# A kernel's prologue re-ordered: shorter TensorE filler, two x pieces summed together, the R4 sum moved ahead, transposes of group 1 moved ahead

## The chip, the core and the metric

The kernel runs on one core of a Trainium2 chip. The metric is the device time of one execution in microseconds (us). Five runs of the kernel before took 325.96, 326.41, 326.27, 325.49 and 325.08 us: median 325.96. One more execution was profiled; it took 325.05 us by the same clock. Below, TensorE is PE, VectorE is DVE, ScalarE is ACT, GpSimd is POOL, SyncE is SP. PEld is the loading of weights into TensorE, which the profile lists apart from the matmul.

## What is computed

Eight sequences (batches) of 4224 positions with 192 channels go through a causal convolution with softmax-normalised taps, then through a mixing block: a low-rank mix over the positions, and a two-layer network over the channels.

```python
w = softmax(weight, axis=-1)                       # 8 heads x 7 taps, 24 channels a head
y[b,s,h*24+g] = sum_k w[h,k] * x[b, s+k-6, h*24+g] # zero before the start
h = U^T y  (32 x 192), then  V^T h                 # rank 32 over the 4224 positions
u = y + V^T (U^T y)
out = u + relu(u @ w_ch1) @ w_ch2                  # 192 -> 768 -> 192
```

Inputs are float32; x, U, V and both channel weights are turned to bf16 by the transfers that load them, sums are held in float32, and the output is float32.

## The kernel before

A batch is 33 tiles of 128 positions, all eight batches 264 tiles, in 33 groups of 8 tiles. In steady work a group goes through three stages: `h_group` (V^T h from TensorE, added to y by DVE, giving u), a transpose of u, `w1` (36 matmuls of 512 columns, whose results pass through relu on ACT and DVE), and four calls of `w2` (24 narrower matmuls each pair of tiles, whose results DVE adds to u before SP stores them). The schedule is written out by hand: every engine runs its instructions in the order of the program, so what stands earlier in the text stands earlier in the queue. The list `SLOTS` orders everything after the prologue; the change does not touch it. It touches the prologue, which gets batch 0 from nothing to the first `w1`.

The names that matter there, with the lines of the kernel before:

- **x of batch 0** comes in four pieces (`KP`, L86, `x_piece`). A batch's x lies as two halves of 64 partitions, r = 0 (tiles 0 to 15) and r = 1 (tiles 16 to 32). Pieces 0 and 1 are the first ten tiles of each half, piece 2 the last 7 tiles of half 1, piece 3 the last 6 of half 0. POOL issues all loads (L79).
- **Filler**: `idle` (L153) multiplies a zeroed float32 tile `zz` (128x512, zeroed by DVE at L145) by its own first 128 columns. Each call appears as two passes in the trace. `idle(5)` stands first in TensorE's queue, `idle(1)` between the two band halves. Nothing reads the result.
- **The band matrices**: the convolution is a matmul with a banded weight matrix. DVE works from the taps to two products `pr` (L208), one for four heads each; `band_half` (L228) sums the 7 taps of one product on TensorE, and ACT (half 0) or DVE (half 1) copies the band out of PSUM in four pieces.
- **conv** (L351) computes the convolution for some heads and some tiles, and evicts the result to `y_sb`, an SBUF tile.
- **tt** is U^T y. `tt_mm` (L391) sums over tiles in four column strips of the array, four tiles at a time; the four partial sums are split into a bf16 head and rest (`tt_split`), and a matmul with `R4` adds the four and repeats the sum on all four strips. `tt_late` (L674) takes a tile by itself with the weights repeated four times over (`U4_sb`, made by POOL at L700), straight into the bank `ps0` where the final sum lies; it needs no R4. `tt_done` (L415) copies the sum to SBUF as `tt_sb`.
- **Groups 0 and 1** don't use the DMA transpose. `yT_part` (L498) transposes y of a piece of a group by matmuls with the identity; `hT_part` (L512) adds the transposed V^T h into the same PSUM bank, and evicts the sum to `uT`, the input of `w1`.

The order on TensorE before, after the first convolution: the U layout (L260), the first transposes of group 0, convolution of piece 2, `tt_mm` of the 20 tiles of pieces 0 and 1, convolution of piece 3, `tt_late` of the 7 tiles of piece 2, R4, `tt_late` of the 6 tiles of piece 3, the last transposes of group 0, `hT_part` of group 0, all transposes of group 1, `hT_part` of group 1, and then `w1` of group 0.

PSUM has 8 banks, handed out in turn by `bank()`.

Of the kernel before, what the change touches and what calls it, by code (L numbers as in the profile page):

```python
# [9 lines left out]
BF16 = mybir.dt.bfloat16  # L10
F32 = mybir.dt.float32
# [3 lines left out]
def kernel(  # L15
# [10 lines left out]
    nc = tc.nc  # L26
    P = nc.NUM_PARTITIONS
    B, S, D = x.shape
    H, KC = weight.shape
    GS = D // H  # L30
    R = moe_U.shape[1]
    M4 = moe_w_ch1.shape[1]
    NT = S // P
# [11 lines left out]
    cst = ctx.enter_context(tc.tile_pool(name="cst", bufs=1))  # L45
# [10 lines left out]
    def bank():  # L56
        return psp.tile([P, 512], F32, name="ps", tag="ps")
# [9 lines left out]
    NB0 = 32  # L67
    NB1 = S // HB - NB0
# [7 lines left out]
    def x_part(b, r, s0, s1):  # L76

        blk = NB0 * r + s0 - 1
        return nc.gpsimd.dma_start(  # L79
            out=xt[b][HB * r : HB * r + HB, s0:s1, :],  # L80
            in_=x[b, blk * HB : (blk + s1 - s0) * HB, :].rearrange("(j p) d -> p j d", p=HB),
        )

    XP = [(0, 1, 17), (0, 17, NB0 + 1), (1, 0, 18), (1, 18, NB1 + 1)]

    KP = [(0, 0, 10), (1, 0, 10), (1, 10, NB1 // 2), (0, 10, NB0 // 2)]  # L86

    def x_piece(k):
        r, k0, k1 = KP[k]
        x_part(0, r, (1 - r if k0 == 0 else 2 * k0 + 1), 2 * k1 + 1)  # L90

    def piece_tiles(k):
        r, k0, k1 = KP[k]
        return [NB0 // 2 * r + j for j in range(k0, k1)]

    x_tile(0)
    for k in range(2):
        x_piece(k)


    I32 = mybir.dt.int32
# [25 lines left out]
    )  # L127
    nlast = NT * 32 - nfull * P
    nc.gpsimd.dma_start(out=Ur[0:nlast, nfull, :], in_=U4[nfull * P :, :])
    for k in range(2, len(KP)):  # L130
        x_piece(k)


# [3 lines left out]
    for m0, m1 in ((0, 2 * P), (2 * P, M4)):  # L137
        for hf in range(2):
            nc.gpsimd.dma_start(
                out=W1_sb[HB * hf : HB * hf + HB, :, m0:m1],  # L140
                in_=moe_w_ch1[:, m0:m1].rearrange("(c k) m -> k c m", k=HB),
            )

    zz = cst.tile([P, 512], F32, name="zz")
    nc.vector.memzero(zz[:])  # L145

    rq = cst.tile([P, 2], F32, name="rq")
# [2 lines left out]
            nc.vector.memset(rq[QB * r : QB * r + QB, n : n + 1], v * r)  # L150
    wps = bank()

    def idle(n):  # L153
        for _ in range(n):
            nc.tensor.matmul(out=wps[:], lhsT=zz[:, 0:P], rhs=zz[:], start=True, stop=True)  # L155

    idle(5)

# [95 lines left out]
    def u_layout(up):  # L256
        nb = [nfull + (1 if 32 * jj < nlast else 0) for jj in range(4)]
        for a in range(4):
            for jj in range(4):
                nc.tensor.matmul(  # L260
                    out=up[jj][:, 0 : nb[jj] * R],
                    lhsT=Eq[32 * jj : 32 * jj + 32, a, :],
                    rhs=Ur[32 * jj : 32 * jj + 32, 0 : nb[jj], a * R : (a + 1) * R],
                    start=(a == 0),
                    stop=(a == 3),
                    tile_position=(32 * jj, 0),
                )
        for jj in range(4):
            evac(
                "AD"[jj % 2],  # L270
                U_sb[:, 0 : nb[jj], jj, :],
                up[jj][:, 0 : nb[jj] * R].rearrange("p (k r) -> p k r", r=R),
            )

    band_half(0)
    idle(1)
    band_half(1)


# [68 lines left out]
                    pp[part][:, 0 : nk[part] * GS].rearrange("p (k a) -> p k a", a=GS),  # L348
                )

    def conv(b, h0, nh, rs, engs, k0=0, k1=NT, pp=None):  # L351

        if yt[b] is None:
            yt[b] = ys.tile([P, NT, D], BF16, name="y_sb")
        nk = {r: min(k1, (NB0, NB1)[r] // 2) - k0 for r in rs}
        if pp is None:
            pp = {r: bank() for r in rs}
        w = nh * GS
        for hh in range(nh):
            h = h0 + hh  # L360
            for halo in range(2):
                for r in rs:
                    for c in range(2):
                        st = 1 - halo + c + 2 * k0
                        last = nc.tensor.matmul(  # L365
                            out=pp[r][HB * c : HB * c + HB, 0 : nk[r] * w].rearrange(
                                "p (k a) -> p k a", a=w
                            )[:, :, hh * GS : hh * GS + GS],
                            lhsT=bands[h // HQ][
                                HB * r : HB * r + HB, h % HQ, HB * halo : HB * halo + HB  # L370
                            ],
                            rhs=xt[b][
                                HB * r : HB * r + HB,
                                st : st + 2 * nk[r] - 1 : 2,
                                h * GS : h * GS + GS,
                            ],
                            start=(halo == 0),
                            stop=(halo == 1),
                            tile_position=(HB * r, HB * c),
                        )  # L380
        for n, r in enumerate(rs):
            j0 = NB0 // 2 * r + k0
            evac(
                engs[n % len(engs)],
                yt[b][:, j0 : j0 + nk[r], h0 * GS : h0 * GS + w],
                pp[r][:, 0 : nk[r] * w].rearrange("p (k a) -> p k a", a=w),
            )
        return last
# [3 lines left out]
    def tt_mm(b, js, p=None):  # L392

        if p is None:
            p = bank()
        for n, j in enumerate(js):
            c = n % 4
            nc.tensor.matmul(  # L398
                out=p[32 * c : 32 * c + 32, 0:D],
                lhsT=U_sb[:, j // 4, j % 4, :],  # L400
                rhs=yt[b][:, j, :],
                start=(n < 4),
                stop=(n + 4 >= len(js)),
                tile_position=(0, 32 * c),
            )
        return p

    def tt_split(b, p):

        hi = sml.tile([P, D], BF16, name="tt_hi")  # L410
        lo = sml.tile([P, D], BF16, name="tt_lo")
        nc.scalar.activation(out=hi[:], in_=p[:, 0:D], func=ACT.Copy)  # L412
        nc.vector.tensor_tensor(out=lo[:], in0=p[:, 0:D], in1=hi[:], op=ALU.subtract)
        ttb[b] += [hi, lo]
# [84 lines left out]
    def yT_part(g, parts):  # L499


        for c, i0, i1, p, _ in parts:
            for i in range(i0, i1):
                for hf in range(2):
                    nc.tensor.matmul(  # L505
                        out=p[HB * hf : HB * hf + HB, (i - i0) * P : (i - i0 + 1) * P],
                        lhsT=yt[0][:, GT * g + 4 * hf + i, HB * c : HB * c + HB],
                        rhs=ident[:],
                        start=(i == i0),
                        stop=False,  # L510
                        tile_position=(0, HB * hf),
                    )  # L512
# [156 lines left out]
        LOADS[b] = [(g, 0), (g, 3), (g + 1, 0), (g + 1, 3)]  # L669


    late = [piece_tiles(k) for k in (2, 3)]
    U4_sb = cst.tile([P, sum(len(js) for js in late), 4, R], BF16, name="U4_sb")

    def tt_late(p, js, o, first, last):

        for n, j in enumerate(js):
            nc.tensor.matmul(  # L678
                out=p[:, 0:D],
                lhsT=U4_sb[:, o + n, :, :].rearrange("p a r -> p (a r)"),  # L680
                rhs=yt[0][:, j, :],
                start=first and n == 0,
                stop=last and n + 1 == len(js),
            )

    def conv_piece(k, pps):
        r, k0, k1 = KP[k]
        for n, h in enumerate(range(0, H, 3)):
            conv(0, h, min(3, H - h), [r], "AD"[n % 2], k0, k1, {r: pps[n]})

    for h in range(0, H, 2):
        conv(0, h, 2, [0, 1], "AA" if h == 0 else "AD", *KP[0][1:])
    work = [bank() for _ in range(4)]
    u_layout(work)
    x_tile(1)
    x_zero(1, nc.gpsimd)
    x_part(1, *XP[0])
    o = 0
    for js in late:
        nc.gpsimd.tensor_copy(  # L700
            out=U4_sb[:, o : o + len(js), :, :],
            in_=U_sb[:]
            .rearrange("p k j r -> p (k j) r")[:, js[0] : js[-1] + 1, :]
            .unsqueeze(2)
            .to_broadcast([P, len(js), 4, R]),
        )
        o += len(js)

    NSL = (NT + 7) // 8 * 2
    V_sb = cst.tile([P, NSL, P], BF16, name="V_sb")  # L710
# [13 lines left out]
    W2_sb = cst.tile([P, MC, D], BF16, name="W2_sb")  # L724
    nc.gpsimd.dma_start(out=W2_sb[:], in_=moe_w_ch2[:].rearrange("(m p) d -> p m d", p=P))

    ps0 = bank()
    parts0 = [(0, 0, 2, bank(), "A"), (0, 2, 4, bank(), "D"), (1, 0, 4, bank(), "D")]
    yT_part(0, parts0)
    conv_piece(2, work[0:3])  # L730
    tt_mm(0, piece_tiles(0) + piece_tiles(1), work[3])
    tt_split(0, work[3])
    conv_piece(3, work[0:3])
    tt_late(ps0, late[0], 0, True, False)
    for part in ttb[0]:
        nc.tensor.matmul(out=ps0[:, 0:D], lhsT=R4[:], rhs=part[:], start=False, stop=False)
    tt_late(ps0, late[1], len(late[0]), False, True)
    more = [(2, 0, 2, bank(), "A"), (2, 2, 4, bank(), "A")]
    yT_part(0, more)
    tt_done(0, ps0)  # L740
    hT_part(0, parts0 + more)
    parts1 = [(c, 0, 4, bank(), "ADA"[c]) for c in range(3)]
    yT_part(1, parts1)
    hT_part(1, parts1)
    band2 = cst.tile([P, H, QB], BF16, name="band2")
    for xp in XP[1:]:
        x_part(1, *xp)
# [92 lines left out]
```

## Time and profile before

| | |
|---|---|
| median of 5 runs | 325.96 us (325.08 to 326.41) |
| the profiled execution | 325.05 us, of which the span from the first to the last recorded instruction is 323.3 us |
| outside the span | 1.75 us |
| DVE busy | 268.9 us (83%) |
| ACT busy | 170.4 us (53%) |
| POOL busy | 143.5 us (44%) |
| from 9.88 to 20.35 us (batch 0 up to the first `w1`) | PE 10.47 of 10.47 us busy, DVE 6.40, ACT 6.67, POOL 8.19; 194 GB/s moved |
| from 81 us on, each batch | about 28.1 us, PE busy throughout |

How to read it: a share of busy time is an average. The chain of waits says what set the end: it is followed back from the last instruction, step by step, to what released it. In the listings, a row gives the start in us from the span's beginning, the length in us, the engine, the line of the kernel, the operation, what it writes and reads, and how many; in brackets stands how long the engine sat idle ahead of it, and what ended that. A matmul's recorded length includes its way through the array, so rows overlap; the distance from start to start is what one costs in a stream.

### The profile page before, as it was taken

To read this page: it belongs to the slowest core of one execution; us is meant where nothing else is said; L and a number is where in the kernel's file an instruction comes from. 1 tells how busy PE (TensorE), PEld (TensorE's weight loads), DVE (VectorE), ACT (ScalarE), POOL (GpSimd) and SP (SyncE) were. 2 spreads that over 40 slices of the span, in tenths; PEclk is the share of its full clock that TensorE was granted. 3 is DMA by queue.
4 is the path that set the end of the run, shared out by engine and by line. 5 is a ranking of instruction groups with operands and counts; after the bars stand their busy time and mean duration, and the time that the engine had idled before them with its cause. 6 is when DMAs were issued, how large, how long until landed. Compare 5 with 4: busy or idle time off the path is not lost.

```text
span 323.3 us, 9590 instructions
## 1 busy us (share of the span) xinstructions
PE 318.1 (98%) x3998; PEld 224.0 (69%) x3998; DVE 268.9 (83%) x551; ACT 170.4 (53%) x344; POOL 143.5 (44%) x112
## 2 busy tenths in 40 slices
PE   8999999999999999999999999999999999999996
PEld 3757576478677647867864784587797497487495
DVE  7769989987977986998798699879888897896864
ACT  1766723860874397088339608824903902912920
POOL 8774179728957694785859497000000000000000
PEclk9999999999999999999999999999999999999999
DMA  9999993998998999699799957139269059048035
GB/s 104 193 192 183 207 212 101 190 194 257 211 134 202 226 175 172 168 153 199 171 235 150 223 150 196 37 111 242 58 170 270 3 149 269 25 121 271 2 120 175
DMA packets 122907, 53.52 MB, mean 166 GB/s; under 512 B 87760, under 2 KB 122832, under 8 KB 122864
## 3 DMA queue, kind: packets, MB, share of 16 engines
q1 hardware_dynamic: 84528, 38.08, 47.1%
q0 software_dynamic: 38192, 14.73, 40.1%
q8 instruction: 31, 0.51, 0.6%
q14 instruction: 12, 0.10, 0.1%
q10 hardware_dynamic: 144, 0.10, 0.1%
HBM read 29.49 MB, written 25.95 MB: 171 GB/s over the span
## 4 chain that ended last, share of the span: by engine, by line
PE 92%; ACT 3%; DMA 2%; DVE 1%; issue 0%; POOL 0%; POOLq 0%
PE ps L579 42%; PE ps L550 39%; PE ps L335 3%; PE ps L453 3%; DMA x_sb<-in_x_dram 2%; PE ps L398 2%; ACT rl_sb L564 2%; PE ps L365 1%; ACT y_sb L252 1%; PE ps L505 1%; DVE u_sb L475 1%; DVE rl_sb L566 1%; PE ps L520 0%; PE ps L678 0%; PE ps L424 0%
## 5 line engine op out<-in xcount | busy, mean ns | idle before, releaser
L564 ACT ACTIVATE rl_sb<-ps 128x512 bf16<-128x512 f32 x233 | 124.3, 604 | 108.0 <-PE ps L550 96.0
L579 PE MATMUL ps<-W_sb,rl_sb 128*128 128x192 bf16 x1584 | 141.9, 246 | 0.2
L579 PEld LDWEIGHTS <-rl_sb 128*128 128x128 bf16 x1584 | 128.1, 98 | 13.5 <-issue 13.1
L550 PE MATMUL ps<-uT,W_sb 64*128 64x512 bf16 x1188 | 131.7, 376 | 0.0
L566 DVE TENSOR_SCALAR rl_sb<-ps 128x512 bf16<-128x512 f32 x163 | 105.2, 686 | 15.7 <-PE ps L550 15.4
L550 PEld LDWEIGHTS <-W_sb 64*128 64x128 bf16 x1188 | 66.9, 94 | 60.5 <-issue 3.8
L588 DVE TENSOR_TENSOR out_sb<-ps,u_sb 128x384 f32<-128x384 f32 (+1 forms) x133 | 70.3, 548 | 25.9 <-PE ps L579 25.5
L301 POOL COPY xb_sb<-x_sb 32x3072 bf16<-32x3072 bf16 (+1 forms) x24 | 67.5, 2824 | 0.7
L475 DVE TENSOR_TENSOR u_sb<-y_sb,ps 128x192 bf16<-128x192 bf16 (+1 forms) x168 | 66.2, 459 | 0.0
L289 POOL COPY xb_sb<-x_sb 128x3072 bf16<-128x3072 bf16 x12 | 32.7, 2744 | 34.5 <-PE ps L335 24.8
L252 ACT ACTIVATE y_sb<-ps 128x384 bf16<-128x384 f32 (+4 forms) x90 | 38.2, 515 | 10.8 <-PE ps L335 7.8
L79 POOL DMA_DIRECT2D x_sb<-in_x_dram x32 | 27.0, 847 | 17.2 <-PE ps L550 10.4
L254 DVE CAST y_sb<-ps 128x408 bf16<-128x408 f32 (+4 forms) x36 | 19.1, 577 | 1.3 <-PE ps L365 1.1
L453 PE MATMUL ps<-tt_sb,V_sb 32*128 32x192 bf16 x264 | 12.4, 246 | 0.1
L335 PE MATMUL ps<-x_sb,band 64*32 64x384 bf16 x192 | 12.1, 333 | 0.0
L335 PE MATMUL ps<-xb_sb,band 64*32 64x384 bf16 x192 | 12.1, 332 | 0.0
L453 PEld LDWEIGHTS <-V_sb 32*128 32x128 bf16 x264 | 4.7, 92 | 7.3 <-issue 7.3
L155 PE MATMUL ps<-zz 128*128 128x512 f32 x12 | 7.2, 746 | 1.5 <-DVE zz L145 1.5
L365 PE MATMUL ps<-x_sb,band 64*64 64x240 bf16 (+3 forms) x192 | 8.0, 276 | 0.2 <-DMA x_sb<-in_x_dram 0.2
L412 ACT ACTIVATE tt_hi<-ps 128x192 bf16<-128x192 f32 x8 | 2.6, 330 | 10.6 <-PE ps L398 10.5
L335 PEld LDWEIGHTS <-band 64*32 64x32 bf16 x384 | 4.5, 89 | 4.1 <-issue 3.0
L365 PEld LDWEIGHTS <-band 64*64 64x64 bf16 x192 | 5.9, 106 | 2.2 <-issue 1.6
(65 smaller groups left out, 73.3 us busy)
## 6 DMA issues: line engine op xcount, KB each, us to landing
out_dram<-out_sb SPq DMA_DIRECT2D x131, 192.0 KB, 2.8
x_sb<-in_x_dram POOLq DMA_DIRECT2D x14, 384.0 KB, 7.6
x_sb<-in_x_dram POOLq DMA_DIRECT2D x7, 432.0 KB, 8.4
x_sb<-in_x_dram POOLq DMA_DIRECT2D x7, 408.0 KB, 7.6
x_sb<-in_x_dram POOLq DMA_DIRECT2D x1, 504.0 KB, 7.6
uT<-u_sb SPq DMA_TRANSPOSE x31, 4.0
x_sb<-in_x_dram POOLq DMA_DIRECT2D x1, 480.0 KB, 5.9
W_sb<-in_moe_w_ch_dram POOLq DMA_DIRECT2D x2, 192.0 KB, 7.5
```

Of the source, the lines that this page charges most:

```text
L79: return nc.gpsimd.dma_start(out=xt[b][HB * r : HB * r + HB, s0:s1, :], in_=x[b, blk * HB : (blk + s1 - s0) * HB, :].rearrange("(j p) d -> ...
L252: nc.scalar.activation(out=out, in_=in_, func=ACT.Copy)
L289: nc.gpsimd.tensor_copy(out=xbt[b][:, s0:s1, :], in_=xt[b][:, s0 + 1 : s1 + 1, :])
L301: nc.gpsimd.tensor_copy(out=xbt[b][q, s0:s1, :], in_=xt[b][q, s0:s1, :])
L335: nc.tensor.matmul(out=pp[r][QB * cg : QB * cg + QB, 0 : nk[r] * GS], lhsT=w[hr], rhs=t[hr, st : st + 2 * nk[r] - 1 : 2, hs], start=True, ...
L453: nc.tensor.matmul(out=banks[pr][:, a * D : (a + 1) * D], lhsT=V_sb[32 * q : 32 * q + 32, (j // 8) * 2 + j % 2, :], rhs=ttb[b][32 * q : 32 ...
L475: nc.vector.tensor_tensor(out=u_group(g)[:, i : i + n, :, hf, :], in0=yt[b][:, run[0] : run[0] + n, :].rearrange("p n (c k) -> p n c k", c=3),
L550: last = nc.tensor.matmul(out=pps[m][hf][:], lhsT=W1_sb[HB * hf : HB * hf + HB, c, m * P : (m + 1) * P], rhs=uTt[g][HB * hf : HB * hf + HB ...
L564: nc.scalar.activation(out=rl[:, m, hf, :], in_=pp[hf][:], func=ACT.Relu)
L566: nc.vector.tensor_scalar_max(out=rl[:, m, hf, :], in0=pp[hf][:], scalar1=0.0)
L579: last = nc.tensor.matmul(out=cps[:, a * D : (a + 1) * D], lhsT=rlt[g][:, m, hf, (i + a) * P : (i + a + 1) * P], rhs=W2_sb[:, m, :], start ...
L588: nc.vector.tensor_tensor(out=o[:, 0:n, :].rearrange("p n (c k) -> p n c k", c=3), in0=cps[:, 0 : n * D].rearrange("p (n c k) -> p n c k", ...
```

## The change

Five edits, all in the prologue.

1. The zero tile `zz` shrinks from 128x512 to 128x128, and the filler reads it four times over by a broadcast. `idle(5)` becomes `idle(4)`; the filler between the band halves is half as wide (256 columns).
2. Pieces 0 and 1 become one entry of `KP`; the four loads stay, in the same order.
3. `tt_mm` now takes 27 tiles: the 7 tiles of the third piece join the 20. `U4_sb` holds 6 tiles in place of 13, so one POOL copy goes (128x896; the one of 128x768 stays).
4. The R4 sum now opens the bank of the final sum, ahead of the late tiles; `tt_late` of 6 tiles follows. The final sum lies in `work[3]`, and `tt_mm` gets a bank `tp` of its own.
5. Of the last transposes of group 0, one half (4) goes between R4 and `tt_late`, the other stays behind it; 8 of the 24 transposes of group 1 move from behind `hT_part` of group 0 to in front of it.

On the engines other than TensorE, but for that one POOL copy, the order and number of the instructions stay as they were.

```diff
-    KP = [(0, 0, 10), (1, 0, 10), (1, 10, NB1 // 2), (0, 10, NB0 // 2)]
+    KP = [{0: (0, 10), 1: (0, 10)}, {1: (10, NB1 // 2)}, {0: (10, NB0 // 2)}]
...
-    zz = cst.tile([P, 512], F32, name="zz")
+    zz = cst.tile([P, P], F32, name="zz")
     nc.vector.memzero(zz[:])
...
-    def idle(n):
+    def idle(n, w=4):
         for _ in range(n):
-            nc.tensor.matmul(out=wps[:], lhsT=zz[:, 0:P], rhs=zz[:], start=True, stop=True)
-
-    idle(5)
+            nc.tensor.matmul(
+                out=wps[:, 0 : w * P].rearrange("p (n t) -> p n t", t=P),
+                lhsT=zz[:],
+                rhs=zz[:].unsqueeze(1).to_broadcast([P, w, P]),
+                start=True,
+                stop=True,
+            )
+
+    idle(4)
...
     band_half(0)
-    idle(1)
+    idle(1, 2)
     band_half(1)
...
-    late = [piece_tiles(k) for k in (2, 3)]
-    U4_sb = cst.tile([P, sum(len(js) for js in late), 4, R], BF16, name="U4_sb")
+    late = piece_tiles(2)
+    U4_sb = cst.tile([P, len(late), 4, R], BF16, name="U4_sb")
...
     work = [bank() for _ in range(4)]
+    tp = bank()
     u_layout(work)
...
-    ps0 = bank()
     parts0 = [(0, 0, 2, bank(), "A"), (0, 2, 4, bank(), "D"), (1, 0, 4, bank(), "D")]
     yT_part(0, parts0)
-    conv_piece(2, work[0:3])
-    tt_mm(0, piece_tiles(0) + piece_tiles(1), work[3])
-    tt_split(0, work[3])
-    conv_piece(3, work[0:3])
-    tt_late(ps0, late[0], 0, True, False)
-    for part in ttb[0]:
-        nc.tensor.matmul(out=ps0[:, 0:D], lhsT=R4[:], rhs=part[:], start=False, stop=False)
-    tt_late(ps0, late[1], len(late[0]), False, True)
+    conv_piece(1)
+    tt_mm(0, piece_tiles(0) + piece_tiles(1), tp)
+    tt_split(0, tp)
+    conv_piece(2)
+    ps0 = work[3]
+    for n, part in enumerate(ttb[0]):
+        nc.tensor.matmul(out=ps0[:, 0:D], lhsT=R4[:], rhs=part[:], start=(n == 0), stop=False)
     more = [(2, 0, 2, bank(), "A"), (2, 2, 4, bank(), "A")]
-    yT_part(0, more)
+    yT_part(0, more[0:1])
+    tt_late(ps0)
+    yT_part(0, more[1:])
+    parts1 = [(0, 0, 4, bank(), "A")]
+    yT_part(1, parts1)
     tt_done(0, ps0)
     hT_part(0, parts0 + more)
-    parts1 = [(c, 0, 4, bank(), "ADA"[c]) for c in range(3)]
-    yT_part(1, parts1)
-    hT_part(1, parts1)
+    rest = [(c, 0, 4, bank(), "ADA"[c]) for c in (1, 2)]
+    yT_part(1, rest)
+    hT_part(1, parts1 + rest)
```

More of the change, by code (lines that the diff above doesn't have):

```diff
@@ L84 @@
     XP = [(0, 1, 17), (0, 17, NB0 + 1), (1, 0, 18), (1, 18, NB1 + 1)]
-    KP = [(0, 0, 10), (1, 0, 10), (1, 10, NB1 // 2), (0, 10, NB0 // 2)]
+    KP = [{0: (0, 10), 1: (0, 10)}, {1: (10, NB1 // 2)}, {0: (10, NB0 // 2)}]
     def x_piece(k):
-        r, k0, k1 = KP[k]
-        x_part(0, r, (1 - r if k0 == 0 else 2 * k0 + 1), 2 * k1 + 1)
+        for r, (k0, k1) in KP[k].items():
+            x_part(0, r, (1 - r if k0 == 0 else 2 * k0 + 1), 2 * k1 + 1)
     def piece_tiles(k):
-        r, k0, k1 = KP[k]
-        return [NB0 // 2 * r + j for j in range(k0, k1)]
+        return [NB0 // 2 * r + j for r, ks in KP[k].items() for j in range(*ks)]
     x_tile(0)
-    for k in range(2):
-        x_piece(k)
+    x_piece(0)
     I32 = mybir.dt.int32
@@ L129 @@
     nc.gpsimd.dma_start(out=Ur[0:nlast, nfull, :], in_=U4[nfull * P :, :])
-    for k in range(2, len(KP)):
+    for k in range(1, len(KP)):
         x_piece(k)
@@ L349, in conv32, with conv @@
                 )
-    def conv(b, h0, nh, rs, engs, k0=0, k1=NT, pp=None):
+    def conv(b, h0, nh, rs, engs, ks=((0, NB0 // 2), (0, NB1 // 2)), pp=None):
         if yt[b] is None:
             yt[b] = ys.tile([P, NT, D], BF16, name="y_sb")
-        nk = {r: min(k1, (NB0, NB1)[r] // 2) - k0 for r in rs}
+        nk = {r: ks[r][1] - ks[r][0] for r in rs}
         if pp is None:
@@ L363, in conv @@
                     for c in range(2):
-                        st = 1 - halo + c + 2 * k0
+                        st = 1 - halo + c + 2 * ks[r][0]
                         last = nc.tensor.matmul(
@@ L381, in conv @@
         for n, r in enumerate(rs):
-            j0 = NB0 // 2 * r + k0
+            j0 = NB0 // 2 * r + ks[r][0]
             evac(
@@ L669, with tt_late @@
         LOADS[b] = [(g, 0), (g, 3), (g + 1, 0), (g + 1, 3)]
-    late = [piece_tiles(k) for k in (2, 3)]
-    U4_sb = cst.tile([P, sum(len(js) for js in late), 4, R], BF16, name="U4_sb")
-    def tt_late(p, js, o, first, last):
-        for n, j in enumerate(js):
+    late = piece_tiles(2)
+    U4_sb = cst.tile([P, len(late), 4, R], BF16, name="U4_sb")
+    def tt_late(p):
+        for n, j in enumerate(late):
             nc.tensor.matmul(
                 out=p[:, 0:D],
-                lhsT=U4_sb[:, o + n, :, :].rearrange("p a r -> p (a r)"),
+                lhsT=U4_sb[:, n, :, :].rearrange("p a r -> p (a r)"),
                 rhs=yt[0][:, j, :],
-                start=first and n == 0,
-                stop=last and n + 1 == len(js),
-            )
[L686 to L689, printed above, removed]
+                start=False,
+                stop=(n + 1 == len(late)),
+            )
     for h in range(0, H, 2):
-        conv(0, h, 2, [0, 1], "AA" if h == 0 else "AD", *KP[0][1:])
+        conv(0, h, 2, [0, 1], "AA" if h == 0 else "AD", KP[0])
     work = [bank() for _ in range(4)]
+    tp = bank()
     u_layout(work)
@@ L698 @@
     o = 0
-    for js in late:
+    for r, (k0, k1) in KP[2].items():
+        j = NB0 // 2 * r + k0
         nc.gpsimd.tensor_copy(
-            out=U4_sb[:, o : o + len(js), :, :],
+            out=U4_sb[:, o : o + k1 - k0, :, :],
             in_=U_sb[:]
-            .rearrange("p k j r -> p (k j) r")[:, js[0] : js[-1] + 1, :]
+            .rearrange("p k j r -> p (k j) r")[:, j : j + k1 - k0, :]
             .unsqueeze(2)
-            .to_broadcast([P, len(js), 4, R]),
+            .to_broadcast([P, k1 - k0, 4, R]),
         )
-        o += len(js)
+        o += k1 - k0
     NSL = (NT + 7) // 8 * 2
@@ L725, with conv_piece @@
     nc.gpsimd.dma_start(out=W2_sb[:], in_=moe_w_ch2[:].rearrange("(m p) d -> p m d", p=P))
-    ps0 = bank()
     parts0 = [(0, 0, 2, bank(), "A"), (0, 2, 4, bank(), "D"), (1, 0, 4, bank(), "D")]
     yT_part(0, parts0)
-    conv_piece(2, work[0:3])
-    tt_mm(0, piece_tiles(0) + piece_tiles(1), work[3])
-    tt_split(0, work[3])
-    conv_piece(3, work[0:3])
-    tt_late(ps0, late[0], 0, True, False)
-    for part in ttb[0]:
-        nc.tensor.matmul(out=ps0[:, 0:D], lhsT=R4[:], rhs=part[:], start=False, stop=False)
-    tt_late(ps0, late[1], len(late[0]), False, True)
-    more = [(2, 0, 2, bank(), "A"), (2, 2, 4, bank(), "A")]
-    yT_part(0, more)
+    def conv_piece(k):
+        for n, h in enumerate(range(0, H, 3)):
+            for r in KP[k]:
+                conv(0, h, min(3, H - h), [r], "AD"[n % 2], KP[k], {r: work[n]})
+    conv_piece(1)
[5 more added lines that the diff above has]
+        nc.tensor.matmul(out=ps0[:, 0:D], lhsT=R4[:], rhs=part[:], start=(n == 0), stop=False)
+    more = [(2, 0, 2, bank(), "A"), (2, 2, 4, bank(), "A")]
+    yT_part(0, more[0:1])
[3 more added lines that the diff above has]
+    yT_part(1, parts1)
     tt_done(0, ps0)
     hT_part(0, parts0 + more)
-    parts1 = [(c, 0, 4, bank(), "ADA"[c]) for c in range(3)]
-    yT_part(1, parts1)
-    hT_part(1, parts1)
+    rest = [(c, 0, 4, bank(), "ADA"[c]) for c in (1, 2)]
+    yT_part(1, rest)
+    hT_part(1, parts1 + rest)
     band2 = cst.tile([P, H, QB], BF16, name="band2")
```

## The prediction

> **What bounds the kernel now.** First the page's busy times and its chain of waits:
>
> ```profile
> PE 318.1 (98%) x3998; PEld 224.0 (69%) x3998; DVE 268.9 (83%) x551; ACT 170.4 (53%) x344; POOL 143.5 (44%) x112
> PE 92%; ACT 3%; DMA 2%; DVE 1%; issue 0%; POOL 0%; POOLq 0%
> ```
>
> TensorE's own work is 92% of the chain that sets the end. From 81 us on PE is busy throughout, so what the prologue saves on TensorE should arrive at the end, and what it saves elsewhere is worth nothing. So next the chain in order of time, for the first 45 us (start, length, what):
>
> ```profile
> 1.25 1.02 POOL x_sb L79
> 2.27 7.56 DMA x_sb<-in_x_dram
> ...
> 9.88 1.94 PE ps L365 x62
> 11.82 0.77 PE ps L260 x15
> 12.59 0.73 PE ps L505 x16
> 13.31 1.28 PE ps L365 x32
> 14.59 0.53 PE ps L398 x20
> 15.12 1.12 PE ps L365 x32
> 16.23 0.69 PE ps L678 x7
> 16.92 0.17 PE ps L736 x2
> 17.08 0.49 PE ps L678 x6
> 17.58 0.51 PE ps L505 x8
> 18.09 0.78 PE ps L520 x10
> 18.87 0.79 PE ps L505 x24
> 19.66 0.76 PE ps L520 x6
> 20.42 1.23 PE ps L550 x10
> ```
>
> The reader is to see two things. Up to 9.83 us the second x load holds the chain, not the band and not the filler; then TensorE runs without a gap to w1 at 20.42. Last, the filler's rows by tile (min/median/max ns) and the timeline around its end:
>
> ```profile
> L155 PEld LDWEIGHTS ps<-zz x12: 190/192/337, 1.5 to 7.9; 128*128 128x128 f32 x12
> L155 PE MATMUL ps<-zz x12: 592/592/1222, 1.5 to 8.4; 128*128 128x512 f32 x12
> 7.42 0.62 PE L232 MATMUL ps<-pr,ident 128*128 128x152 bf16 x7
> 8.79 0.62 PE L232 MATMUL ps<-pr,ident 128*128 128x152 bf16 x7
> ```
>
> **Filler and bands.** Ten filler passes run from 1.47 to 7.42. In the timeline they start at 2.48, 3.33, 4.19 (0.86 apart), then 4.85, 5.28, 5.71, 6.13 (0.43 apart): TensorE doubles its speed at about 4.65, since the weight loads halve as well (337 to 190 ns). The granted-clock column says 1.00 throughout and does not show this. The product for half 0 is there at about 7.3 (two products, 6.04 to 8.48, half each), so in this execution the filler delays half 0 by some 0.1. Half 1 starts at 8.79, its product ends at 8.48: 0.3 too late, of which DVE gives back little, being busy until 9.32 with other constants; its copies started at 9.45 and would start at 9.36. The second half of the first convolution waits for these copies (PEld idle 0.17 until the band), so it gains 0.09. But the third x piece was issued at 5.70 and landed 7.5 later, at 13.2, and its convolution began at 13.24: 0.00 to 0.09 is left. I take 0.04.
>
> **Other executions.** [...] The five runs reach from 325.08 to 326.41, median 325.96, and the profiled one, which switched early, took 325.05: 0.9 under the median. [...] With the change: clearing 128 columns in place of 512 takes about 0.17 in place of 0.485 (slope from the 256-column clears, 0.275 each), so passes start at 1.16; eight of them end at 6.4 if the speed doubles at 4.65, and at 8.1 at the latest (all slow). The half-width filler takes 0.43 at full speed. [...]
>
> [...]
>
> **27 tiles, R4 ahead.** Seven tiles in four strips cost 0.53/20 = 27 ns each, 0.19; as late tiles they cost 0.58 (16.17 to 16.75 in the timeline). They need the last eviction of their convolution piece, though (ACT, ends 15.09, against PE free at about 15.05): about 0.1 of wait. So the last convolution piece starts at 15.40 and ends at 16.52 in place of 16.23. R4 (0.17), then 4 transposes at 0.79/24 = 33 ns (0.13): 16.82. Now the 6 late tiles wait for the last eviction, which before started 0.05 behind the convolution and took 0.41: ready at 17.03, 0.2 of new wait on TensorE, with everything queued behind it. They end at 17.53 against 17.58. **Of the 0.39 saved on late tiles 0.05 is left**, because the eviction of the last piece is late next. The head/rest split on ACT and DVE moves 0.3 later and pushes the evictions behind it, which fit: DVE 15.84 to 16.2, then its copy 0.61, ready at 16.9.
>
> **Transposes of group 1.** Between the end of the late tiles and hT lies 0.51 (17.58 to 18.09), set by DVE's copy of the sum (0.36 and two hand-overs). Eight transposes of group 0 lay under it, 0.27. Now 12 do (4 and 8), 0.40: still covered, end at 17.93 against 18.04. Behind hT 16 remain in place of 24: **8 x 33 = 0.27 saved**. If that cover went, it would return as cost.
>
> **POOL and queues.** One copy goes: 896 of 1664 columns of 1.69 us, 0.91. The V loads behind it may issue that much sooner, at most; 4 x 64 KB is 1.35 us of traffic at 194 GB/s. That could push the last w_ch1 load, which landed at 11.78 + 7.2 = 19.0, to 19.5 at worst; w1 needs it after 21. The last V load waits for a w_ch1 load and stays at 17.74, landing at 23.4; h of group 2 would run at about 24.0 in place of 24.34. Covered, by 0.6. The x loads of batch 1 land at 31 and are used at 37.65. SP's order is unchanged. Each broadcast pass streams as many columns as before: nothing.
>
> **Sum** against the profiled execution: 0.04 + 0.05 + 0.27 = 0.36 (bounds 0.1, if the new waits double, and 0.6, if the evictions come as early as now); 325.05 - 0.36 = 324.7. From there I see no stage that takes it back: relu on ACT bounds 21.65 to 24.69, but starts when w1 starts. If the phase explains the runs, their median falls near the same value, plus 0.1 for late phases and landings: **324.8, 1.2 below 325.96**.
>
> **The cases.** A measurement of this kernel can tell about 0.3% (1.0 us) from no change.
>
> - *As forecast, 53%*: 324.8, own range 324.3 to 325.2.
> - *The phase doesn't matter, 27%*: spread has another source (transfer landings), only the sum counts: 325.96 - 0.36 = 325.6. For it: a single trace shows one switch; DMA engines are busy from 4 us on. Against: 0.9 between median and profiled run.
> - *The clock isn't open when the convolution starts, 12%*: one mechanism. [...]
> - *It doesn't do what it says, 8%*: the new waits on evictions take the whole 0.36 and the runs' spread stays: 326.0.
>
> A quarter of the first case and nearly all of the second and fourth lie within 0.3%. Faster by over 0.3% (below 324.98): three quarters of 53% and a little of the second, 0.44. Slower: 0.13. The rest, 0.43. The range leaves out the slow clock and the lower tail: 324.2 to 326.0.
>
> **What would show it.** In the trace after: filler starts at about 1.16 and TensorE has a gap ahead of the first band half; the second half begins near 8.5; the first convolution still begins when the x load lands; an idle of 0.1 ahead of the 21st tile of the 27 and 0.2 ahead of the late tiles, ended by ACT's eviction; w1 begins near 20.1. The five times should lie closer together than 1.3 us. Wrong if w1 begins no sooner, if band matmuls run at half pace, or if the times spread as before.

## The result and the profile after

The changed kernel takes 325.26 us (median of 28 runs, 325.02 to 327.12); the kernel before, run beside it, 325.42 us (47 runs, 324.80 to 327.99). Ratio 0.9995, 95% interval 0.9985 to 1.0006: no change that can be told. Under the median two things moved. The middle half of the runs drew together, from 325.05 to 326.08 before to 325.15 to 325.54 after; and the lowest time rose, from 324.80 to 325.02. One edit won, and another part of the change gave it back.

The profiled execution took 326.86 us, one of the slowest. The page's busy times and chain:

```profile
PE 318.1 (98%) x3996; PEld 221.7 (68%) x3996; DVE 268.5 (83%) x551; ACT 170.6 (52%) x344; POOL 142.8 (44%) x111
PE 87%; DMA 5%; DVE 3%; ACT 3%; issue 1%; POOL 0%; SPq 0%; DVEq 0%; POOLq 0%
```

PE is busy for the same time to 0.1 us. The chain's larger DMA share comes from one place far behind the change, seen in the chain in order of time:

```profile
71.57 0.04 SPq L600
...
71.70 7.75 DMA out_dram<-out_sb
```

That store took 7.75 us, against a median of 2.8, and DVE then waited for an output buffer. All other traces of this study have 304.70 to 304.74 us from the first matmul of w1 (in the timeline, where it starts 0.07 ahead of the chain's row) to the end of the time; this one has 306.13. So 1.4 us of it is this event, which no other trace repeats, and **for everything else the start of w1 tells the time**. The same view for the prologue:

```profile
2.28 7.60 DMA x_sb<-in_x_dram
9.88 0.04 issue
9.93 1.83 PE ps L369 x62
...
13.36 1.28 PE ps L369 x32
14.64 0.53 PE ps L402 x20
15.16 0.02 issue
15.18 0.34 PE ps L402 x7
15.53 1.12 PE ps L369 x32
16.65 0.27 PE ps L741 x2
16.92 0.23 PE ps L509 x4
17.15 0.04 issue
17.19 0.57 PE ps L682 x5
17.77 0.17 issue
17.93 0.24 PE ps L682
18.17 0.46 PE ps L509 x12
18.63 0.83 PE ps L524 x10
19.46 0.57 PE ps L509 x16
20.03 0.76 PE ps L524 x6
20.79 1.23 PE ps L554 x10
```

w1 starts at 20.79, not at 20.1, and later than the 20.42 of before. From the start of the third x piece's convolution, c3 for short (13.31 before, 13.36 here; ahead of it the landing of x sets the pace), it is 7.11 before and 7.43 now. The late tiles (L682) show why: five follow each other, then 0.17 of "issue", and only then the sixth, on whose sum DVE's copy and everything behind it wait. From start to start the fifth and sixth lie 0.41 apart; a late tile costs 0.08.

Two theories had to be tested. **C** (clock): the shorter filler makes the bands independent of the moment at which TensorE's speed doubles (4.64 in the trace of before, 4.07 in the changed kernel's). **F** (fetch): the gap is TensorE running out of instructions, at a fixed place of its stream. Rivals to F: **W**, a wait of the sixth tile for data; **S**, the loss lies only in the added switches of the array's tiling.

### The profile page after: what moved, and what is told of

Same layout as the page of the kernel before. It is cut to its first block, busy times and chain, and to the rows that moved or that the text cites. A ratio compares the mean times of both kernels' runs of the same rounds, so it can differ in the third digit from the quotient of the medians.

```text
span 325.0 us, 9584 instructions
## 1 busy us (share of the span) xinstructions
PE 318.1 (98%) x3996; PEld 221.7 (68%) x3996; DVE 268.5 (83%) x551; ACT 170.6 (52%) x344; POOL 142.8 (44%) x111
## 4 chain that ended last, share of the span: by engine, by line
PE 87%; DMA 5%; DVE 3%; ACT 3%; issue 1%; POOL 0%; SPq 0%; DVEq 0%; POOLq 0%
PE ps L583 39%; PE ps L554 38%; PE ps L339 3%; PE ps L457 3%; DMA out_dram<-out_sb 2%; DMA x_sb<-in_x_dram 2%; PE ps L402 2%; ACT rl_sb L568 2%; DVE u_sb L479 2%; PE ps L369 1%; ACT y_sb L256 1%; DVE out_sb L592 1%; DVE rl_sb L570 1%; PE ps L509 1%; PE ps L524 0%
## 5 line engine op out<-in xcount | busy, mean ns | idle before, releaser
L554 PEld LDWEIGHTS <-W_sb 64*128 64x128 bf16 x1188 | 65.0, 94 | 62.9 <-issue 4.5
L79 POOL DMA_DIRECT2D x_sb<-in_x_dram x32 | 27.1, 850 | 13.3 <-PE ps L554 6.6
L402 PE MATMUL ps<-y_sb,U_sb 128*32 128x192 bf16 x258 | 7.4, 247 | 0.0
```

Of the source, the lines that this page charges most:

```text
L79: return nc.gpsimd.dma_start(out=xt[b][HB * r : HB * r + HB, s0:s1, :], in_=x[b, blk * HB : (blk + s1 - s0) * HB, :].rearrange("(j p) d -> ...
L554: last = nc.tensor.matmul(out=pps[m][hf][:], lhsT=W1_sb[HB * hf : HB * hf + HB, c, m * P : (m + 1) * P], rhs=uTt[g][HB * hf : HB * hf + HB ...
```

## The experiments

The first four kernels were timed beside 51 runs of before (median 325.35 us), the last four beside 53 (325.51 us). "w1 behind c3" is the time in the trace from the first matmul of c3 to the first of w1; before 7.11.

| kernel | runs | lowest | median | middle half | ratio to before | w1 behind c3 |
|---|---|---|---|---|---|---|
| filler_only | 14 | 324.76 | 325.05 | 324.99 to 325.21 | 0.9994 (0.9982 to 1.0007) | 7.11 |
| order_only | 22 | 325.22 | 325.53 | 325.42 to 326.00 | 1.0014 (0.9999 to 1.0030) | 7.13 |
| halves_behind | 14 | 324.88 | 325.01 | 324.95 to 325.08 | 0.9992 (0.9977 to 1.0008) | 7.15 |
| pad16 | 14 | 324.86 | 325.65 | 325.06 to 325.79 | 1.0005 (0.9992 to 1.0018) | 7.10 |
| after_again | 13 | 325.06 | 325.19 | 325.13 to 325.33 | 0.9998 (0.9979 to 1.0017) | 7.39 |
| halves_pad8 | 14 | 324.98 | 325.47 | 325.13 to 325.66 | 0.9990 (0.9976 to 1.0005) | 7.25 |
| filler_c0 | 15 | 324.72 | 324.83 | 324.80 to 324.97 | 0.9981 (0.9972 to 0.9990) | 6.98 |
| no_filler | 20 | 325.25 | 326.12 | 325.64 to 326.56 | 1.0020 (1.0007 to 1.0033) | 7.11 |

Most intervals reach across 1, since the middle half of before is itself about 0.9 us wide; below, the traces carry the reading and the medians go beside them.

**filler_only**: before, with the first edit alone.

```diff
-    idle(5)
+    idle(4)
...
-    idle(1)
+    idle(1, 2)
```

> The kernel before with the first edit alone (smaller zero tile, 4 fillers in place of 5, a half-wide one between the band halves). Theory C (the filler holds the bands up in those executions where TensorE's speed doubles late): the first convolution starts when the x load lands in every execution, so the times lie within 0.8 us of each other and the median falls by about 0.5, to 324.9. Rival (the spread has another source, transfers): median and spread as before, 325.4 and 324.8 to 326.4. Theory F (TensorE's instruction stream runs dry at a fixed place, see the next run): four instructions fewer stand ahead, so the gap of 0.2 among the 8 transposes moves two transposes later, and w1 begins at 20.3 to 20.4.

As C has it: 13 of 14 times lie within 0.6 us (the other is 327.20), and the median is 325.05, less of a fall than the 324.9 expected. The floor hardly moves (324.76; before, timed beside it, 324.88), the upper half goes. The edit has three parts, a shorter clearing of `zz`, one filler less and a narrower one between the halves; no run takes them apart. As for F, the gap stands two transposes later, as expected, but is 0.05 long, and w1 began at 20.25.

**order_only**: the changed kernel with the old filler (the diff of filler_only turned round).

> The changed kernel with the filler of before (5 fillers, 512 columns, a full one between the halves): edits 2 to 5 alone. Theory F: the gap of 0.41 ahead of the sixth late tile comes from TensorE's instruction fetch and stands at a fixed count of instructions; four more stand ahead of it here, so it moves to the fourth late tile, and w1 begins at 20.7 to 20.8, as in the changed kernel. Rival W (the sixth late tile waits for an eviction or for its weights): the gap stays at the sixth. Theory C: the times spread over 1.3 us again, with a floor near 325.0 and a median near 325.8; without C the median is 325.2 to 325.4 with the narrow spread of the changed kernel.

Its trace happened to catch a late doubling. TensorE's timeline, then DVE's:

```profile
1.47 6.64 PE L153 MATMUL ps<-zz 128*128 128x512 f32 x10 [1.47 <-DVE zz L143]
7.94 0.62 PE L230 MATMUL ps<-pr,ident 128*128 128x152 bf16 x7
9.31 0.62 PE L230 MATMUL ps<-pr,ident 128*128 128x152 bf16 x7
...
11.33 1.01 PE L363 MATMUL ps<-x_sb,band 64*64 64x240 bf16 x30 [0.36 <-DVE band L252]
```

```profile
9.97 1.30 DVE L252 CAST band<-ps 32x152 bf16<-32x152 f32 x4 [0.64 <-PE ps L230]
```

The passes last 6.64 in place of 6.12, both band halves come 0.52 later than in the first trace (7.42 and 8.79), and now the convolution waits 0.36 for DVE's band, where it had been waiting for x. That is the loss which theory C supposes, seen, though in part made up again: of the 0.52, 0.18 is left at c3 (13.42 against 13.24 in the timeline). The median of 325.53, with a middle half 0.58 wide, lies between C's 325.8 and the 325.2 to 325.4 expected without C. That the longer times of before itself come from late doublings was not traced; it is inferred, since they go with the edit. Of F, the gap has moved to the fourth late tile as expected, but is 0.03 long, and w1 began at 20.62.

**halves_behind**: the changed kernel, transposes of group 0 back behind the late tiles.

```diff
-    yT_part(0, more[0:1])
     tt_late(ps0)
-    yT_part(0, more[1:])
+    yT_part(0, more)
```

> The changed kernel with the four transposes of group 0 that stood between R4 and the late tiles put back behind them. Theory S (a switch of the array's tiling between kinds of matmul costs 0.15 to 0.18 each, and the four transposes add two): R4 to late tile costs 0.08 again, and the late tiles are bound by ACT's last eviction. Theory F: the same number of instructions stands ahead of the gap, which now falls on the third transpose behind the late tiles and no longer on the sum; the copy of the sum starts at 17.65 in place of 18.21, w1 at 20.4 to 20.5 in place of 20.73, median about 325.0. Rival W: the gap stays with the sixth late tile, w1 at 20.7.

Here the speed doubled later still: the eight passes last 6.38, until 7.4, against 5.17 in the changed kernel's trace. With the new filler this costs nothing (TensorE's timeline):

```profile
1.07 6.38 PE L153 MATMUL ps<-zz 128*128 128x512 f32 x8 [1.07 <-DVE zz L143]
7.36 0.62 PE L236 MATMUL ps<-pr,ident 128*128 128x152 bf16 x7
...
8.54 0.62 PE L236 MATMUL ps<-pr,ident 128*128 128x152 bf16 x7
...
9.75 0.50 PE L369 MATMUL ps<-x_sb,band 64*64 64x240 bf16 x12 [0.37 <-DMA x_sb<-in_x_dram]
...
17.01 0.66 PE L682 MATMUL ps<-y_sb,U_sb 128*128 128x192 bf16 x6 [0.28 <-ACT y_sb L256]
```

Compare the second band half: 8.54 here and 9.31 in order_only. The last row shows the late tiles held by ACT's last eviction, as the prediction had it. No gap is left in this trace, and w1 comes 7.15 behind c3; the median is 325.01, 0.25 under the changed kernel's. Rival S finds no support: the first late tile starts 3.90 behind the first matmul of c3 here and in the changed kernel alike, so the two added switches delay nothing.

**pad16**: the changed kernel with four tiny float32 matmuls behind the first filler, 16 instructions in the stream.

```diff
     idle(4)
+    for _ in range(4):
+        nc.tensor.matmul(
+            out=wps[0:QB, 0:8], lhsT=zz[:, 0:QB], rhs=zz[:, 0:8], start=True, stop=True
+        )
```

> The changed kernel with four tiny float32 matmuls (sixteen instructions in the stream) added in the gap that TensorE has ahead of the bands, where they cost no time of their own. Theory F: the gap moves eight matmuls earlier, from the sixth late tile to the second or third of the four transposes behind R4, and is not shorter than before; w1 begins at 20.7 to 21.0. Rivals W and S: the place of the gap and w1 at 20.73 stay as they are. Median 325.2 to 325.5.

The gap left the sixth tile, against W; but none appeared at the new place, where F had expected one, and w1 came 7.10 behind c3, 0.3 sooner than in the changed kernel. The times fall in two clusters, 324.86 to 325.08 and 325.64 to 326.27 (and one of 327.33); the trace (325.06) is of the first, so what makes the second stays open.

**after_again**: the changed kernel, unchanged.

> The changed kernel once more, beside the next runs. Theory F (TensorE's instruction fetch is a race: it is asked for at a fixed place of the stream and lands about 2.4 us later, so the gap has the length by which TensorE comes too early): a gap of 0 to 0.4 ahead of the sixth late tile and nowhere else near, w1 begins 7.1 to 7.45 behind the convolution of the third x piece, median 325.25. If the gap in the first trace was a chance event: none here, 7.1, and the median above that of halves_behind needs another cause.

The chain in order of time has the gap at the same tile, and w1 7.39 behind c3:

```profile
17.12 0.57 PE ps L682 x5
17.69 0.12 issue
17.81 0.24 PE ps L682
```

**halves_pad8**: halves_behind with two of the tiny matmuls, 8 instructions, where TensorE waits for x.

```diff
     band_half(1)
+    for _ in range(2):
+        nc.tensor.matmul(
+            out=wps[0:QB, 0:8], lhsT=zz[:, 0:QB], rhs=zz[:, 0:8], start=True, stop=True
+        )
```

> halves_behind with two tiny float32 matmuls (eight instructions) between the second band half and the first convolution, where TensorE waits for x anyway. Theory F: the place at which the stream can run dry moves four matmuls earlier, from the fourth transpose behind the late tiles to the sixth late tile itself, so the sum is late again: median 325.2 to 325.3 against 325.01, with a gap of 0 to 0.4 ahead of the sixth late tile in the trace. Rival S (what halves_behind won came from the two switches of the array's tiling alone): the median stays at 325.0.

The gap is back on the sixth late tile, which starts 0.18 behind the fifth. In TensorE's timeline the six tiles last 0.75, against 0.66 in halves_behind:

```profile
16.89 0.75 PE L686 MATMUL ps<-y_sb,U_sb 128*128 128x192 bf16 x6 [0.28 <-ACT y_sb L256]
```

The median is 0.46 above that of halves_behind, more than F asked, but before, timed beside each, differs by 0.16, and the ratio to before shows no rise (0.9990 against 0.9992). This trace, at 324.98 us, is the quickest of its runs, so it does not show the rest; the padding itself may have a share in it.

All traces together: the start of the first 16 KB packet of the instruction queue (q8), the moment at which TensorE would have gone on at the place in question (the 446th of the instructions in the trace, weight loads and matmuls counted alike; a float32 matmul is two of each), the gap, and the time from the packet's start to TensorE's going on, in us.

```
kernel         packet   place reached   gap    packet to go-on
before          15.39   17.51           0.20   2.32
changed         15.50   17.60           0.33   2.43
after_again     15.35   17.53           0.29   2.46
order_only      15.08   17.57           0.03   2.52
filler_only     15.20   17.42           0.05   2.27
filler_c0       15.13   17.37           0.05   2.30
halves_pad8     15.10   17.30           0.10   2.30
halves_behind   15.38   17.68           none
pad16           14.35   16.79           none
no_filler       15.88   18.80           none
```

In seven traces, of six kernels, the gap stands at the 446th instruction, wherever that falls: on the second transpose before, on the sixth or fourth late tile, on the fourth transpose. It ends 2.3 to 2.5 us behind the packet's start; the three traces without a gap reach the place 2.30, 2.44 and 2.92 behind it. On the sum the gap costs its whole length: 0.33 and 0.29 in the two traces of the changed kernel put w1 at 7.43 and 7.39, where pad16, with the same order and no gap, has 7.10; 0.10 in halves_pad8 puts it at 7.25, where halves_behind has 7.15. The trace of before had it too, 0.20 long; there it fell on transposes under DVE's copy of the sum, and cost nothing (7.11, as in filler_only with 0.05). Theory F holds for the place; W falls. The page of the changed kernel has 31 packets of 0.51 MB together for q8, of kind "instruction", so 16 KB each, and 3996 matmuls and as many weight loads for TensorE, some 8000 instructions. That q8 serves TensorE is inferred from these counts, and that the packet is what TensorE waits for from the times; no run changed the packet itself. The moment of the packet's start is not at a fixed count: between 320 and 374 instructions had begun by then. And the size of the effect on the medians is shown less well than its place.

**filler_c0**: filler_only and, of the fifth edit, only the eight transposes of group 1 moved ahead of hT of group 0.

```diff
     yT_part(0, more)
+    parts1 = [(0, 0, 4, bank(), "A")]
+    yT_part(1, parts1)
     tt_done(0, ps0)
     hT_part(0, parts0 + more)
-    parts1 = [(c, 0, 4, bank(), "ADA"[c]) for c in range(3)]
-    yT_part(1, parts1)
-    hT_part(1, parts1)
+    rest = [(c, 0, 4, bank(), "ADA"[c]) for c in (1, 2)]
+    yT_part(1, rest)
+    hT_part(1, parts1 + rest)
```

> The kernel before with the first edit and of the fifth edit only the move of 8 transposes of group 1 to the front of hT of group 0; R4, the late tiles and the 20-tile sum as before. TensorE has 0.12 to spare there beside the switch; the eight add 0.21 to 0.25 in front and take 0.22 away behind. If the cover is as the trace of filler_only has it, w1 begins 0.1 sooner against the convolution of the third x piece (7.0 in place of 7.11), median 324.95. If the copy of the sum doesn't cover them: 7.1, 325.05.

w1 comes 6.98 behind c3, and the median of 324.83 beats both kernels: ratio to before 0.9981 (0.9972 to 0.9990), the filler's gain included, and 0.36 us under the changed kernel timed beside it (after_again). The chain in order of time:

```profile
16.87 0.49 PE ps L684 x6
17.36 0.62 PE ps L511 x16
17.98 0.77 PE ps L526 x10
18.75 0.57 PE ps L511 x16
19.32 0.76 PE ps L526 x6
20.08 1.23 PE ps L556 x10
```

Sixteen transposes stand under the copy of the sum for 0.62, where eight had 0.51; the sixteen behind cost 0.57 in place of 0.79. Net 0.11, a gap of 0.05 included: of all that was tried with the order, only this move gained. halves_behind differs from this kernel only by the 27-tile sum with R4 ahead (edits 2 to 4), and has 7.15: **the 27-tile sum with R4 ahead costs 0.17**.

**no_filler**: the changed kernel without any filler.

```diff
-    idle(4)
...
-    idle(1, 2)
```

> The changed kernel without any filler; nothing that the output needs is left out. Theory C: TensorE is still at half speed when the bands are made at 7.4 and when the convolution starts, until about 3 us to 6.5 us of work behind 7.4; w1 begins 1.5 to 3 us later, median 326.7 to 328.3. Rival (the filler is of no use, the halved speed belongs to the start of the program): w1 at 20.4 and a median near 325.2.

The median is 326.12, 0.9 above after_again. TensorE's timeline:

```profile
9.52 3.46 PE L367 MATMUL ps<-x_sb,band 64*64 64x240 bf16 x64
```

The first convolution takes 3.46 in place of about 1.9; from the U layout on the pace is normal. So the filler is of use, but the loss is below the expected 1.5 to 3: the slow stretch ended within this convolution (the trace's record of the granted clock begins at 12.72, 5.3 behind the first band matmul), and of the 1.2 by which it ends later than in the changed kernel, 0.4 is made up ahead of c3, which started at 14.1 in place of 13.3. Its w1 comes 7.11 behind c3 although the order is the changed kernel's: with 20 instructions fewer ahead, the 446th lies among the transposes behind the late tiles, and no gap shows.

## Why the prediction was right or wrong

The range held because it reached up to no change: 325.26 is 0.46 above the likeliest value, 324.8, and none of the four cases came out as written. The runs drew together, as in the first; new waits took the order's saving, as in the fourth. That the time fell inside is owed to the width of the range more than to the sum: by the prediction's own sign, "Wrong if w1 begins no sooner", the half on the order failed, since w1 began 0.37 later (20.79 against 20.42). Step by step:

- **Filler and bands, other executions: right in mechanism, too large.** The changed kernel's two traces have the doubling at 4.07 and 5.45, the nine traces with a filler between about 4.1 and 7.1, that is 3.0 to 6.0 behind the first pass. So the same kernel meets it at different moments; what sets them, no run shows. With the old filler a late one moves the bands (order_only, where the second half starts at 9.31 in place of 8.79), with the new one it doesn't (halves_behind; in every trace with the new filler the second half starts at 8.53 or 8.54). But the gain was read from the median of five runs, 325.96, against one trace at 325.05, 0.9 apart. With 47 runs the median of before is 325.42. The edit is worth about 0.3 in the median (before to filler_only, 325.35 to 325.05; order_only to the changed kernel, 325.53 to 325.26). The 0.1 that the sum adds for late phases, that is late doublings, and landings is shown by no run: with the new filler the second half starts at the same 8.53 or 8.54 however late the doubling.
- **27 tiles, R4 ahead: the step that failed.** The late tiles were to end 0.05 sooner than before. Where no gap disturbs them they end 0.22 later, counted from c3: 4.49 in halves_behind (17.67 less 13.18) and in pad16 (17.79 less 13.30), against 4.27 before (17.58 less 13.31). The largest part of this miss of 0.27 lies in "They end at 17.53", which allows the six tiles 0.50 from their start at 17.03. That is the chain's 0.49, which counts from the end of the matmul ahead; from the first one's start to the last one's end, the timeline of before has 0.66:

```profile
16.92 0.66 PE L678 MATMUL ps<-y_sb,U_sb 128*128 128x192 bf16 x6
```

Behind a wait no other matmul hides the first one's way through the array, and the six cost the full 0.66, as the row of halves_behind shows: 0.16 of the miss. Another 0.08 is the last piece's convolution, which starts 0.36 later (15.53 less 13.36, against 15.12 less 13.31) and not 0.28: the 21st tile starts 0.27 behind the 20th, where rows of four tiles lie 0.08 apart, so the wait there is 0.19 and not 0.1. The rest, about 0.03, is the hand-over from ACT.
- **The four transposes behind R4: mispriced, without effect.** "R4 (0.17), then 4 transposes (0.13)" took 0.50. Transposes were priced at the pace of a long run, 33 ns. But the array is tiled otherwise for the transposes (128*64 in the rows) than for R4 and the late tiles (128*128), and in these traces the first matmul of another tiling comes later: the trace before has 0.175 from the last late tile to the first transpose, where two late tiles lie 0.082 apart, and in the changed kernel the transposes start 0.176 behind R4. Yet this did not make the sum late. ACT's last copy of the convolution sets the late tiles, in the changed kernel (first row) as in halves_behind (second), where nothing stands between:

```profile
16.06 1.04 ACT L256 ACTIVATE y_sb<-ps 128x432 bf16<-128x432 f32 x2 [0.16 <-PE ps L369]
15.88 1.04 ACT L256 ACTIVATE y_sb<-ps 128x432 bf16<-128x432 f32 x2 [0.16 <-PE ps L369]
```

The copies end at 17.10 and 16.92, and the late tiles start 0.09 later in both, at 17.19 and 17.01.
- **A gap that no wait explains.** "They end at 17.53" failed by a further 0.29 to 0.33 in the changed kernel: the sixth late tile has no such row in the profile before, where the gap fell on covered work. The text called the queues harmless after looking at the transfers of data; the instruction queue q8 was left out.
- **Transposes of group 1: right, a little smaller.** Twelve lie under the copy for 0.46, and 16 behind cost 0.57 in place of 0.79: 0.22 against the stated 0.27.
- **Sum.** The order was to save 0.32 (0.05 and 0.27). It loses 0.22 ahead of the sum and wins 0.22 behind it, so it is worth about nothing where no gap falls on the sum (7.10 to 7.15 behind c3 against 7.11), and costs 0.28 to 0.32 where the whole gap does. With the 0.3 that the filler won, this leaves the median where it was. "No stage that takes it back" was right: w1's start carried to the end within 0.04 us in every trace but the one with the slow store.
- **The clock that isn't open**: did not come about in any trace with a filler. With the latest doubling, 7.1 in filler_c0, the eight passes last until 7.7, the bands follow without a gap, and the first convolution's 62 matmuls take 1.94, as before. Only no_filler has the convolution start at the slow pace, and it lost 0.9 in the median.

## What to carry to other kernels

When a change puts a group of short matmuls behind a wait, count it from its first start to its last end, as its row in the timeline has it, and not by its share of a chain in which rows overlap (here 0.66 against 0.49). Count a change of array tiling too (here 0.15 to 0.2 from start to start, against 0.03 to 0.08 within a kind), where no later wait covers it. Keep what the next stage waits for away from a place where the traces show such a gap (here the 446th instruction), or leave covered work there: 0.20 us of it cost nothing on transposes (before), while 0.29 and 0.33 us on the sum cost their whole length (the changed kernel's two traces). And take the size of a gain in spread from many runs: five had put the median 0.5 too high.

## What the runs showed of the hardware

- The instruction queue q8 moved 31 packets of 16 KB, in 0.6% of the time of the 16 DMA engines that also moved the data (9 tenths busy in the page's second and third slices, 8 to 24 us). In the seven traces with a gap TensorE would have gone on at the 446th instruction 2.1 to 2.5 us behind the start of the first packet, and did go on 2.3 to 2.5 us behind it, 0.03 to 0.33 us late. That the two race each other is inferred.
- The granted-clock column shows 1.00 both in the stretch where filler passes lie 0.85 apart (before, up to 4.6) and in the one where they lie 0.43 apart. The trace's records of the granted clock begin only at the doubling (4.64 before, 4.07 in the changed kernel, 12.72 in no_filler; pad16 has none there), and the column reads 1.00 where there is no record. The doubling is to be seen in the distances, in the weight loads (337 to 190 ns) and in the start of the first record.
